# Last query chunk's output product in seven half-size products, and the fourth tile's end moved by one query group

## Chip, cores and metric

The kernel runs on one core of a Trainium2 chip. The metric is device time in microseconds (us) of one execution; where several were timed, their median. The profiled execution is one of them: its span is what the profile shows, from first to last instruction, and a little more lies around it. TensorE (PE in the profile) multiplies matrices, VectorE (DVE) and ScalarE (ACT) work on elements, GpSimd (POOL) and SyncE (SP) issue the DMAs here.

## The reference, cut to what matters

Attention with 16 query heads on 8 key/value heads over the last 512 keys, with a gated feed-forward branch on the same normalised input. The output is `x + s * g`.

```python
# x (1, 2048, 448); Hq = 16, Dh = 256, Hkv = 8, W = 512
xn = layernorm(x)
q  = (xn @ wq).reshape(1, 2048, 16, 256).transpose(0, 2, 1, 3)
p  = softmax(einsum("bhqd,bhkd->bhqk", q, k[last 512]) * 256 ** -0.5)
o  = einsum("bhqk,bhkd->bhqd", p, v[last 512])
s  = o.transpose(0, 2, 1, 3).reshape(1, 2048, 4096) @ wo      # 4096 x 448
g  = silu((gelu(xn @ w_gate) * (xn @ w_up)) @ w_down)
out = x + s * g
```

The change is in the product with `wo`, 2048 x 4096 times 4096 x 448.

## The kernel before

**An order written out by hand.** `Plan` (lines 39 to 166) records every operation in program order. Each engine runs its own operations in that order, and semaphore waits follow from who wrote and who reads each buffer. `K.reuse` (line 61) makes a new buffer wait for all users of the bytes that it overlaps. A DMA is an operation of the engine whose queue issues it: one that has to wait holds back everything behind it on that engine. All matmuls are recorded in line 370, all ScalarE copies in line 361, two-operand VectorE operations in line 364, plain DMAs in line 355 and transposing DMAs in line 358; one goes by tile names.

**Stages.** First comes the normalisation and the feed-forward branch, whose gate `g` goes to DRAM (`g2_all`, in the profile `g_all`) tile by tile, 16 tiles of 128 tokens. Then attention runs over `m` from 0 to 63 (line 906): four chunks of 512 tokens, 16 heads in each. `groups` (line 347) says at which `m` query projections are computed for the next 6 or 8 heads, two heads at a time (`q_group`, line 695). In each chunk after the first they stand at `m % 16 == 2` and `m % 16 == 10`. `s_mm(m)` (line 713) makes the scores of one head in the four banks `AB`, ScalarE takes the exponentials into `p32`, VectorE normalises them into `pn` (three buffers), and SP transposes `pn` into `pT` by DMA, two transposes for a head. `pv(m)` (line 734) multiplies by the values two heads later (`LAG = 2`), in two of the four banks `BB`. Its result goes to `oTh` in half precision, scaled by 64, for chunks 0 to 2, and to `oT` (the same bytes, bfloat16) for chunk 3. In a steady step TensorE does `s_mm(m)` and `pv(m - 2)`.

**The output product of chunks 0 to 2** is `burst(c)` (line 799), called at `m % 16 == 1` of the next chunk. It splits the chunk's tokens, the head dimension and 384 of the 448 output columns in two and needs seven half-size products in place of eight (`product`, line 786, in half precision, with weights `wt` prepared earlier). Four of the seven have sums of `oTh` as their operand; `sums(n)` (line 812) makes them on VectorE for four heads at a time into three buffers `sr`, which lie over `qT`, `pn` and `p32`. The other 64 columns are plain products with `w3` (line 846), in bank `BN`. Results come out transposed. `plus`, `part` and `fold` (lines 823 to 839) put them together in `xs` (the first chunk's columns of `xnT`), SP transposes `xs` by DMA into `sT` and `sN`, and `burst_end(c, t4)` (line 879) finishes a tile of tokens. It is called for tiles 0 to 2 within the query projections at `m % 16 == 2` and for tile 3 at `m % 16 == 3` (line 930).

**The output product of chunk 3** is plain: `wo_mm` (line 750), 32 pieces of the contraction for each of four tiles, the last tile split into 320 and 128 columns (lines 938 to 954). The first two tiles' pieces of heads 0 to 12 stand before or between the last two `pv`. Its weights `wo` (3.5 MB) go over the bytes of `wt` in four loads of 896 KB by POOL's queue (`load_wo`, line 895): two within the burst of chunk 2 (lines 853 and 861), one in the second projection step at m = 50 and one in the first step at m = 58 (line 913).

**The end of a tile** is `wo_end` (line 757), with `wo_fin` (line 772) for chunk 3:

```python
mult(g2[:, g, :], b_g2[g])                       # DVE: product with the gate
if t + NG2 < NT and c1 == D: load_g2(t + NG2)    # POOL queue; NG2 = 2
add("dve", xr[:, x, c0:c1], ...)                 # DVE: plus x
dma("sp" if t >= NT - 4 else "pool", out_view[:, t, c0:c1], xr[:, x, c0:c1], bx, ())
if t + NXR < NT and c1 == D:                     # NXR = 3, POOL queue
    dma("pool", xr[:, x, :], x_view[:, t + NXR, :], (), b_xr[x])
```

There are two buffers for the gate (`g2`) and three for `x` (`xr`, overwritten by the output). Tile 12 ends first in chunk 3, tile 15 last.

Of the kernel before, what the change touches and what calls it, by code (L numbers as in the profile page):

```python
# [168 lines left out]
def bass_recurrent_scan__sliding_block_cached__geglu_ffn__prompt_kernel(  # L169
# [41 lines left out]
    with es:  # L211
# [14 lines left out]
        def sbuf_bufs(at, size, n):  # L226
            return [K.buf(at + i * size, size) for i in range(n)]
# [53 lines left out]
        w3, _, rw_end = place("w3", [P, NCO, R], F16)  # L281
        w3b, _, _ = place("w3b", [P, NCO, R], BF16, at=a_w3)
        b_w3 = [K.buf(a_w3 + i * NCO // NB * R * 2, NCO // NB * R * 2) for i in range(NB)]
        wo, a, a2 = place("wo", [P, NCO, D], BF16, at=rw + 3 * Hq * N2 * 2)
        assert a2 <= rw_end
        b_wo = sbuf_bufs(a, 8 * D * 2, NCO // 8)
        x4, a, a2 = place("x4", [P, NT, D], BF16, at=rw)
        b_x4 = sbuf_bufs(a, D * 2, NT)
        NXN = 14
# [67 lines left out]
        def dma_t(o, i, reads=(), writes=()):  # L357
            K.op("sp", lambda e, o=o, i=i: e.dma_start_transpose(o, i), reads, writes, dma=True)
# [350 lines left out]
                     (b_ps[b + 1],), (b_qT[s][1],))  # L709

        AB, BB = [], []

        def s_mm(m):
            s, g = qs(m), m % Hq // 2
# [19 lines left out]
        def pv(m):  # L734
            h = m % Hq
            g, x = h // 2, m % NPT
            for e in range(2):
                b = BB[m % 2 * 2 + e]
                mms([(bank[b].rearrange("p (t q) -> p t q", q=P), va[:, g, j, e * P:(e + 1) * P],
                      pT[:, x, :, :, j, :].rearrange("p a t q -> p (a t) q"), j == 0, j == NJ - 1)  # L740
                     for j in range(NJ)], [b_va[g]] + b_pT[x], (b_ps[b],))
                i = 2 * h + e
                o, f = (oTh, WS) if m < NS - Hq else (oT, 1.0)
                if e == 0:
                    act(o[:, i, :], bank[b], ACT.Copy, (b_ps[b],), (b_oT[i],), scale=f)
                else:
                    K.op("dve", lambda v, i=i, b=b, o=o, f=f: v.tensor_scalar(  # L747
                        o[:, i, :], bank[b], f, None, op0=ALU.mult), (b_ps[b],), (b_oT[i],))

        def wo_mm(t4, b, lo, hi, c0=0, c1=D):  # L750
            ch = list(range(lo, hi))
            mms([(bank[b][:, c0:c1], oT[:, i, t4 * P:(t4 + 1) * P], wo[:, i, c0:c1], i == 0, i == NCO - 1)
                 for i in ch],
                [b_oT[i] for i in ch] + [b_wo[p] for p in sorted({i // 8 for i in ch})],
                (b_ps[b],))

        def wo_end(t, c0, c1, mult, bt, y):

# [23 lines left out]

        o_view = oTh.rearrange("p (h e) (r q) -> p e r h q", e=2, r=2)
        HALF = (slice(0, R), slice(R, P))

        def product(j, b, rhs, hs, first, reads):

# [11 lines left out]
        def burst(c):  # L799


            allh = list(range(Hq))
            A = lambda e, r: (lambda h: o_view[:, e, r, h, :])
            bA = lambda e, hs: [b_oT[2 * h + e] for h in hs]
            B1, B5, B3, B7 = BB
            B6, BN = AB[0], AB[1]
            F = 0.5 / (WS * WS)
            xs = [xnT[:, k, 0:QC] for k in range(4)]
            U2, U3 = tmp[:, 0, :], tmp[:, 1, :]
            K.reuse([b for x in b_sr for b in x] + [b for x in b_cc[2:] for b in x])  # L810

            def sums(n):
                hs = range(n * HB, (n + 1) * HB)
                t, bt = sr[n % 3], b_sr[n % 3]
                o = lambda e, r: o_view[:, e, r, hs.start:hs.stop, :]
                S = lambda i: t[:, i, :, :]
                for i, x, y, r, op in ((3, o(0, 0), o(0, 1), bA(0, hs), ALU.subtract),
                                       (2, o(1, 1), S(3), bA(1, hs) + [bt[3]], ALU.subtract),
                                       (0, S(2), o(0, 0), bA(0, hs) + [bt[2]], ALU.add),
                                       (1, o(1, 0), S(2), bA(1, hs) + [bt[2]], ALU.subtract)):  # L820
                    add("dve", S(i), x, y, r, (bt[i],), op)
# [18 lines left out]

            for n in range(3):
                sums(n)
            for hs in (allh[:Hq - 2], allh[Hq - 2:]):
                product(0, B1, A(0, 0), hs, hs[0] == 0, bA(0, hs))
            act(U2, bank[B1], ACT.Copy, (b_ps[B1],), b_tmp[0], scale=F)
            for lo, hi in ((0, NCO - 4), (NCO - 4, NCO)):
                mms([(bank[BN][HALF[u], 0:HC], w3[:, i, :], oTh[:, i, u * HC:u * HC + HC], i == 0, i == NCO - 1)
                     for i in range(lo, hi) for u in range(2)],
                    b_oT[lo:hi] + [b_w3[i] for i in sorted({i * NB // NCO for i in range(lo, hi)})], (b_ps[BN],))
            act(xs[3][:, 0:HC], bank[BN][:, 0:HC], ACT.Copy, (b_ps[BN],), b_xs[3:], scale=F)  # L850
            dma_t(sN[:, :, :], xs[3][:, 0:HC], b_xs[3:], (b_sN,))
            if c == NQC - 2:
                load_wo(3)
            for n in range(Hq // HB):
                for j, i, b in ((6, 3, B7), (5, 2, B6), (4, 0, B5), (2, 1, B3)):
                    product(j, b, lambda h, n=n, i=i: sr[n % 3][:, i, h % HB, :], allh[n * HB:(n + 1) * HB], n == 0, [b_sr[n % 3][i]])
                if n == 0:
                    sums(3)
            K.reuse([b for x in b_cc[:2] for b in x])
            if c == NQC - 2:  # L860
                load_wo(0)
            product(1, B1, A(1, 0), allh, False, bA(1, allh))
            part(B1, None, [], 0, 0, 2)
            plus(U2, B6, U2, b_tmp[0], b_tmp[0])
            plus(U3, B7, U2, b_tmp[0], b_tmp[1])
            product(3, B7, A(1, 1), allh, True, bA(1, allh))
            part(B5, U3, b_tmp[1], 1, 1, 3)
            plus(U2, B5, U2, b_tmp[0], b_tmp[0])
            part(B3, U2, b_tmp[0], 0, 1, 0)
            dma_t(sT[:, :, 1, :], xs[1], b_xs[1:2], (b_sT[1],))  # L870
            for r, n, slot in ((0, 0, 2), (1, 1, 3), (0, 1, 0)):
                fold(r, n, slot)
            part(B7, U3, b_tmp[1], 1, 0, 1)
            dma_t(sT[:, :, 0, :], xs[0], b_xs[0:1], (b_sT[0],))
            fold(1, 0, 1)
            dma_t(sT[:, :, 2, :], xs[2], b_xs[2:3], (b_sT[2],))
            K.reuse([b for y in b_qT for b in y])

        def burst_end(c, t4):
# [9 lines left out]
                    add("dve", at(y), i, at(g), reads + [bg], b_tmp[s], ALU.mult)  # L889
            wo_end(t, 0, D, mult, b_tmp[s], y)  # L890

        LAG = 2
        late = []

        def load_wo(i):
            K.reuse(b_wo[i:i + 1])
            dma("pool", wo[:, i * 8:(i + 1) * 8, :],
                A_wo.rearrange("(c p) d -> p c d", p=P)[:, i * 8:(i + 1) * 8, :], (), (b_wo[i],))

        NS = NQC * Hq  # L900
# [4 lines left out]
        BB.extend(bk(nxt, j) for j in range(4))  # L905
        for m in range(NS):
            if m in groups:
                for i in range(m, groups[groups.index(m) + 1], 2):
                    end = m > Hq and m % Hq == LAG
                    q_group(i, (cur, nxt)[((i - m) // 2 + (m == Q0 + QS)) % 2], end)  # L910
                    if end and i > m:
                        burst_end(m // Hq - 1, (i - m) // 2 - 1)
                    if m >= NS - Hq + LAG and i - m == (2 if end else 0):
                        load_wo(1 if end else 2)
                if m == 0:
                    K.reuse([b for x in b_pT for b in x] + b_pn + b_p32)
            if m > Hq and m % Hq == LAG:
                K.reuse(b_pn + b_p32)
            s_mm(m)
            if m < LAG:  # L920
                down(NQC - LAG + m, nxt)
                if m == LAG - 1:
                    K.reuse(b_oT + [b for y in b_qT[:QS - Q0] for b in y])
                    assert not CASTS and not SUMS
                    K.reuse(b_sT + [b_sN])
                    for t in range(NG2):
                        load_g2(t)
            if len(late) == LAG:
                pv(late.pop(0))
            if m > Hq and m % Hq == LAG + 1:  # L930
                burst_end(m // Hq - 1, 3)
            if m > Hq and m % Hq == LAG - 1:
                if m // Hq == 1:
                    for b in b_xs:
                        b.old.extend(y for t in range(4) for z in b_xnT[t] for y in z.readers + [z.writer])
                burst(m // Hq - 1)
            late.append(m)
        c = NQC - 1
        LATE = NCO - 2 * (LAG + 1)
        wo_mm(0, AB[0], 0, LATE)  # L940
        pv(late.pop(0))
        pv(late.pop(0))
        wo_mm(1, AB[1], 0, LATE)
        wo_mm(0, AB[0], LATE, NCO)
        wo_fin(c, 0, AB[0])
        wo_mm(1, AB[1], LATE, NCO)
        wo_fin(c, 1, AB[1])
        wo_mm(2, AB[2], 0, NCO)
        wo_fin(c, 2, AB[2])
        for i in range(2):  # L950
            b = (AB[3], BB[0])[i]
            lo, hi = ((0, CUT), (CUT, D))[i]
            wo_mm(3, b, 0, NCO, lo, hi)
            wo_fin(c, 3, b, lo, hi)

        K.schedule()

# [52 lines left out]
```

## Time and profile before

| what | value |
|---|---|
| median of 5 runs | 560.87 us (560.24 to 562.68) |
| the profiled execution's own time | 560.24 us |
| its span | 558.4 us |
| TensorE busy (matmuls) | 546.6 us, 98% of the span |
| VectorE, ScalarE, GpSimd busy | 346.5, 309.8, 44.6 us |
| mean granted TensorE clock | 0.997 |
| chain that ended last | PE 92%, DMA 4%, DVE 2%, ACT 1%, issue 1% |

The span is divided in 40 slices of 14 us in the page's second part; each digit is the busy share in tenths. The chain that ended last is followed back from the last instruction to what released it at each step. A row of the timeline gives start, length, engine, line, operation and tiles, and in brackets the idle time before it and what ended it. Matmul ends are modelled, so starts are the better measure. A few matmul records are missing. Times below without another word are us from the start of the span.

### The profile page before, as it was taken

How to read it: one execution, taken by the hardware profiler on the slowest of the kernel's cores; microseconds unless marked ns; L12 is line 12 of the kernel's file. 1: busy time of each engine (PE TensorE's matmuls, PEld its weight loads, DVE VectorE, ACT ScalarE, POOL GpSimd, SP SyncE). 2: the span in 40 equal slices, each digit the busy share in tenths (PEclk: the TensorE clock that was granted, in tenths of full speed). 3: DMA queues.
4: the chain of work that ended last, by engine and by line, in shares of the span. 5: the costliest groups of instructions: out<-in, count | busy, mean ns of one | idle time of the engine just before them, and what ended most of it. 6: DMA issues, size and time to landing. Idle time of an engine off the chain costs nothing.

```text
span 558.4 us, 11469 instructions
## 1 busy us (share of the span) xinstructions
PE 546.6 (98%) x4444; PEld 288.5 (52%) x4444; DVE 346.5 (62%) x804; ACT 309.8 (55%) x783; POOL 44.6 (8%) x83
## 2 busy tenths in 40 slices
PE   9999999999999999999999999999999999599997
PEld 5554444445444444974444489444446954244455
DVE  6664635763547758756766795487578747456722
ACT  5434536753558668037857831687586058557700
POOL 1141500000000000003100000310000113100000
PEclk9999999999999999999999999999999999999999
DMA  9666399903307726325943830397076348952702
GB/s 292 121 185 142 87 273 272 162 20 93 87 20 151 151 39 158 37 31 130 166 106 67 161 83 17 79 185 151 14 153 138 97 87 221 183 114 65 144 19 59
DMA packets 177766, 66.46 MB, mean 119 GB/s; under 512 B 159856, under 2 KB 173680, under 8 KB 177712
## 3 DMA queue, kind: packets, MB, share of 16 engines
q1 hardware_dynamic: 172960, 52.76, 45.5%
q0 software_dynamic: 3984, 12.39, 8.2%
q8 instruction: 35, 0.57, 0.5%
q10 hardware_dynamic: 768, 0.57, 0.3%
q14 instruction: 19, 0.16, 0.1%
HBM read 23.43 MB, written 3.67 MB: 49 GB/s over the span
## 4 chain that ended last, share of the span: by engine, by line
PE 92%; DMA 4%; DVE 2%; ACT 1%; issue 1%; ACTq 0%; DVEq 0%
PE bank L370 91%; DMA pT<-pn 4%; ACT p L721 1%; DVE pn L728 1%; PE bank L487 1%; ACT qT L361 0%; DVE oTh L747 0%; DVE rden L725 0%; PE bank L468 0%; DVE tmp L778 0%; DVE xr L364 0%; DVE gl L400 0%; DVE epst L401 0%; ACTq L155 0%; DVE oT L747 0%
## 5 line engine op out<-in xcount | busy, mean ns | idle before, releaser
L721 ACT ACTIVATE p<-bank 128x512 f32<-128x512 f32 x256 | 150.7, 596 | 33.6 <-DVE pn L728 25.8
L370 PE MATMUL bank<-pT,va 128*128 128x512 bf16 x512 | 122.0, 382 | 7.2 <-DMA pT<-pn 7.2
L370 PE MATMUL bank<-kT,qT 128*128 128x512 bf16 x512 | 121.7, 381 | 0.0
L728 DVE TENSOR_SCALAR pn<-p,rden 128x512 bf16<-128x512 f32 x256 | 113.1, 484 | 13.1 <-DMA pT<-pn 8.9
L370 PE MATMUL bank<-xnT,wq 64*128 64x512 bf16 x768 | 94.9, 376 | 0.5 <-DVE oTh L747 0.5
L370 PEld LDWEIGHTS bank<-pT,va 128*128 128x128 bf16 x512 | 49.6, 98 | 69.7 <-DMA pT<-pn 11.1
L370 PE MATMUL bank<-xnT,wgu 64*128 64x512 bf16 (+2 forms) x768 | 83.9, 350 | 0.1
L370 PEld LDWEIGHTS bank<-kT,qT 128*128 128x128 bf16 x512 | 49.6, 98 | 62.9 <-issue 4.8
L361 ACT ACTIVATE qT<-bank 128x512 bf16<-128x512 f32 x76 | 44.1, 596 | 54.1 <-PE bank L370 52.5
L708 DVE CAST qT<-bank 128x512 bf16<-128x512 f32 x52 | 35.1, 692 | 47.5 <-PE bank L370 47.4
L370 PEld LDWEIGHTS bank<-xnT,wq 64*128 64x128 bf16 x768 | 36.7, 94 | 47.1 <-ACT p L721 1.7
L370 PEld LDWEIGHTS bank<-xnT,wgu 64*128 64x128 bf16 x768 | 37.2, 94 | 36.9 <-issue 0.7
L536 DVE TENSOR_TENSOR actT<-bank,gl 128x512 bf16<-128x512 f32 x56 | 37.8, 690 | 26.5 <-PE bank L370 19.9
L361 ACT ACTIVATE gl<-bank 128x512 bf16<-128x512 f32 x56 | 33.2, 597 | 37.0 <-PE bank L370 34.9
L725 DVE RECIPROCAL rden<-rsum 128x2 f32<-128x2 f32 x128 | 21.2, 165 | 50.2 <-ACT p L721 50.0
L721 ACT ACTIVATION_READ_ACCUMULATOR p<-bank 128x1 f32 x256 | 51.4, 201 | 0.0
L370 PE MATMUL bank<-wd,actT 128*128 128x448 bf16 x224 | 43.0, 353 | 0.0
L355 POOL DMA_DIRECT2D g<-g_all x16 | 8.7, 542 | 348.9 <-DVE tmpb L364 285.7
L747 DVE TENSOR_SCALAR oTh<-bank 128x512 f16<-128x512 f32 x48 | 32.8, 683 | 0.0
L370 PEld LDWEIGHTS bank<-wd,actT 128*128 128x128 bf16 x224 | 21.8, 98 | 21.1 <-issue 0.4
L370 PE MATMUL bank<-sr,wt 128*64 128x256 f16 x576 | 31.9, 273 | 0.0
L370 PEld LDWEIGHTS bank<-sr,wt 128*64 128x64 f16 x576 | 31.5, 110 | 0.0
(63 smaller groups left out, 415.9 us busy)
## 6 DMA issues: line engine op xcount, KB each, us to landing
wo<-in_A_wo_dram POOLq DMA_DIRECT2D x4, 896.0 KB, 5.9
wtb<-in_A_wo_dram POOLq DMA_DIRECT2D x4, 768.0 KB, 7.4
wq<-in_A_wq_dram SPq DMA_DIRECT2D x2, 1536.0 KB, 11.3
va<-in_A_v_cache_dram SPq DMA_DIRECT2D x8, 256.0 KB, 5.3
pT<-pn SPq DMA_TRANSPOSE x128, 2.8
g_all<-g2w SPq DMA_DIRECT2D x16, 112.0 KB, 2.1
xr<-in_A_x_dram POOLq DMA_DIRECT2D x16, 112.0 KB, 2.6
g<-g_all POOLq DMA_DIRECT2D x16, 112.0 KB, 2.6
```

The source lines that it names most:

```text
L355: K.op(q, lambda e, o=o, i=i: e.dma_start(o, i), reads, writes, dma=True)
L361: K.op("act", lambda e, o=o, i=i: e.activation(o, i, func, scale=scale), reads, writes)
L370: ins = e.matmul(o, lhsT=l, rhs=r, start=st, stop=sp, skip_group_check=True)
L487: ins = e.matmul(bank[b][:, 0:w], lhsT=gl[:, 0, 0:P], rhs=gl[:, 0, 0:w], start=True, stop=True)
L536: K.op("dve", lambda e: e.tensor_tensor(actT[:, c % 2, f, :], bank[b + 1], gl[:, s, :], ALU.mult), (b_ps[b + 1], b_gl[s]), (b_actT[c % 2][ ...
L708: K.op("dve", lambda v, s=s, b=b: v.tensor_copy(qT[:, s, 1, :], bank[b + 1]), (b_ps[b + 1],), (b_qT[s][1],))
L721: K.op("act", lambda e, b=b, r=r, z=z: e.activation(p32[:, z, :], bank[b], ACT.Exp, scale=att_scale, accum_out=rsum[:, r:r + 1]), (b_ps[b] ...
L725: K.op("dve", lambda e, r=r: e.reciprocal(rden[:, r - 1:r + 1], rsum[:, r - 1:r + 1]), b_rsum[r - 1:r + 1], b_rden[r - 1:r + 1])
L728: K.op("dve", lambda e, r=r - 1 + t, z=(n - 1 + t) % NP32, y=y, t=t: e.tensor_scalar(pn[:, y, t, :], p32[:, z, :], rden[:, r:r + 1], None, ...
L747: K.op("dve", lambda v, i=i, b=b, o=o, f=f: v.tensor_scalar(o[:, i, :], bank[b], f, None, op0=ALU.mult), (b_ps[b],), (b_oT[i],))
```

## The change

The burst is now used for chunk 3 too, for heads 0 to 13. It stands after the loop, ahead of the last two `pv`; there the `w3` product is issued later, behind the seventh product, and the results are not transposed by DMA: `turn` transposes them with small matmuls against `ident` straight into PSUM, and `wo_mm` adds the last two heads' four pieces (`NL = 4`) on top. `wo` is 448 KB and loaded once, by POOL's queue, over the weights of product 0, as soon as that product of the last burst is done. The four `load_wo` are gone. For heads 0 to 13 of chunk 3 `pv` writes scaled half precision. The last burst's factor is 1.0 in place of 0.5, since `wo_fin` multiplies by 0.5. `burst_end(c, 3)` of chunks 0 to 2 goes from m % 16 == 3 to the second projection step at m % 16 == 10. In query groups of six heads (m = 12 and m = 58) the three steps use other PSUM banks.

```diff
@@ placement
-        wo, a, a2 = place("wo", [P, NCO, D], BF16, at=rw + 3 * Hq * N2 * 2)
-        b_wo = sbuf_bufs(a, 8 * D * 2, NCO // 8)
+        NL = 4
+        wo, a, a2 = place("wo", [P, NL, D], BF16, at=rw + WAT[0] * Hq * N2 * 2)
+        b_wo = K.buf(a, NL * D * 2)
@@ pv
-                o, f = (oTh, WS) if m < NS - Hq else (oT, 1.0)
+                o, f = (oTh, WS) if m < NS - LAG else (oT, 1.0)
@@ wo_mm, turn
+        def wo_mm(t4, b, c0=0, c1=D):
+            mms([(bank[b][:, c0:c1], oT[:, i, t4 * P:(t4 + 1) * P], wo[:, i - NCO + NL, c0:c1], False, i == NCO - 1)
+                 for i in range(NCO - NL, NCO)], b_oT[NCO - NL:] + [b_wo], (b_ps[b],))
+
+        def turn(t4, b, c0=0, c1=D):
+            tok = slice(t4 * P, (t4 + 1) * P)
+            lst = [(0, 0, tok, slice(0, P)), (P, 2, tok, HALF[0]), (N2, 1, tok, slice(0, P)), (N2 + P, 2, tok, HALF[1]),
+                   (2 * N2, 3, slice(t4 % 2 * P, t4 % 2 * P + P), HALF[t4 // 2])]
+            lst = [x for x in lst if c0 <= x[0] < c1]
+            mms([(bank[b][:, lo:lo + k.stop - k.start], xs[j][:, q], ident[:, k], i == 0, False)
+                 for i, (lo, j, q, k) in enumerate(lst)], b_xs + [b_ident], (b_ps[b],))
@@ burst
-            allh = list(range(Hq))
+            last = c == NQC - 1
+            NH = Hq - (LAG if last else 0)
+            NCH = 2 * NH
+            allh = list(range(NH))
-            F = 0.5 / (WS * WS)
+            F = (1.0 if last else 0.5) / (WS * WS)
...
-                hs = range(n * HB, (n + 1) * HB)
+                hs = range(n * HB, min((n + 1) * HB, NH))
...
             act(U2, bank[B1], ACT.Copy, (b_ps[B1],), b_tmp[0], scale=F)
-            if c == NQC - 2:
-                load_wo(3)
+            if last:
+                K.reuse([b_wo])
+                dma("pool", wo[:, :, :], A_wo.rearrange("(c p) d -> p c d", p=P)[:, NCO - NL:NCO, :], (), (b_wo,))
+            def plain():
+                for lo, hi in ((0, NCH - 4), (NCH - 4, NCH)):
+                    mms([(bank[BN][HALF[u], 0:HC], w3[:, i, :], oTh[:, i, u * HC:u * HC + HC], i == 0, i == NCH - 1)
+                         for i in range(lo, hi) for u in range(2)],
...
+                act(xs[3][:, 0:HC], bank[BN][:, 0:HC], ACT.Copy, (b_ps[BN],), b_xs[3:], scale=F)
+            def turned(k):
+                if not last:
+                    if k == 3:
+                        dma_t(sN[:, :, :], xs[3][:, 0:HC], b_xs[3:], (b_sN,))
+                    else:
+                        dma_t(sT[:, :, k, :], xs[k], b_xs[k:k + 1], (b_sT[k],))
+            if not last:
+                plain()
+                turned(3)
             for n in range(Hq // HB):
...
-            if c == NQC - 2:
-                load_wo(0)
             product(1, B1, A(1, 0), allh, False, bA(1, allh))
...
             product(3, B7, A(1, 1), allh, True, bA(1, allh))
+            if last:
+                plain()
@@ main loop
-                    q_group(i, (cur, nxt)[((i - m) // 2 + (m == Q0 + QS)) % 2], end)
-                    if m >= NS - Hq + LAG and i - m == (2 if end else 0):
-                        load_wo(1 if end else 2)
+                    p = (i - m) // 2
+                    q_group(i, ((cur, nxt[::-1], (cur[1], nxt[1])) if three else (cur, nxt) * 2)[p], end)
+                    if m > Hq and m % Hq == LAG + QS and p == 1:
+                        burst_end(m // Hq - 1, 3)
-            if m > Hq and m % Hq == LAG + 1:
-                burst_end(m // Hq - 1, 3)
@@ after the loop
+        burst(c)
         pv(late.pop(0))
         pv(late.pop(0))
...
+        ends = [(0, AB[2], 0, D), (1, AB[3], 0, D), (2, AB[0], 0, D), (3, AB[1], 0, CUT), (3, BB[0], CUT, D)]
+        for t4, b, c0, c1 in ends[:3]:
+            turn(t4, b, c0, c1)
+        for i, (t4, b, c0, c1) in enumerate(ends):
+            if i >= 3:
+                turn(t4, b, c0, c1)
+            wo_mm(t4, b, c0, c1)
+            wo_fin(c, t4, b, c0, c1)
```

More of the change, by code (lines that the diff above doesn't have):

```diff
@@ L283, in bass_recurrent_scan__sliding_block_cached__geglu_ffn__prompt_kernel @@
         b_w3 = [K.buf(a_w3 + i * NCO // NB * R * 2, NCO // NB * R * 2) for i in range(NB)]
-        wo, a, a2 = place("wo", [P, NCO, D], BF16, at=rw + 3 * Hq * N2 * 2)
-        assert a2 <= rw_end
-        b_wo = sbuf_bufs(a, 8 * D * 2, NCO // 8)
+        NL = 4
+        wo, a, a2 = place("wo", [P, NL, D], BF16, at=rw + WAT[0] * Hq * N2 * 2)
+        assert NL * D <= Hq * N2
+        b_wo = K.buf(a, NL * D * 2)
         x4, a, a2 = place("x4", [P, NT, D], BF16, at=rw)
@@ L711, in bass_recurrent_scan__sliding_block_cached__geglu_ffn__prompt_kernel @@
         AB, BB = [], []
+        LAG = 2
+        NS = NQC * Hq
         def s_mm(m):
@@ L748, in pv @@
                         o[:, i, :], bank[b], f, None, op0=ALU.mult), (b_ps[b],), (b_oT[i],))
[L750 to L755, printed above, removed]
+        def wo_mm(t4, b, c0=0, c1=D):
[8 more added lines that the diff above has]
+                 for i, (lo, j, q, k) in enumerate(lst)], b_xs + [b_ident], (b_ps[b],))
         def wo_end(t, c0, c1, mult, bt, y):
@@ L784, in bass_recurrent_scan__sliding_block_cached__geglu_ffn__prompt_kernel @@
         HALF = (slice(0, R), slice(R, P))
+        xs = [xnT[:, k, 0:QC] for k in range(4)]
         def product(j, b, rhs, hs, first, reads):
@@ L806, in burst @@
             B6, BN = AB[0], AB[1]
-            F = 0.5 / (WS * WS)
-            xs = [xnT[:, k, 0:QC] for k in range(4)]
+            F = (1.0 if last else 0.5) / (WS * WS)
             U2, U3 = tmp[:, 0, :], tmp[:, 1, :]
@@ L812, in sums @@
             def sums(n):
-                hs = range(n * HB, (n + 1) * HB)
+                hs = range(n * HB, min((n + 1) * HB, NH))
                 t, bt = sr[n % 3], b_sr[n % 3]
                 o = lambda e, r: o_view[:, e, r, hs.start:hs.stop, :]
-                S = lambda i: t[:, i, :, :]
+                S = lambda i: t[:, i, 0:len(hs), :]
                 for i, x, y, r, op in ((3, o(0, 0), o(0, 1), bA(0, hs), ALU.subtract),
@@ L842, in burst @@
                 sums(n)
-            for hs in (allh[:Hq - 2], allh[Hq - 2:]):
+            for hs in (allh[:NH - 2], allh[NH - 2:]):
                 product(0, B1, A(0, 0), hs, hs[0] == 0, bA(0, hs))
             act(U2, bank[B1], ACT.Copy, (b_ps[B1],), b_tmp[0], scale=F)
[L846 to L851, printed above, removed]
-            if c == NQC - 2:
-                load_wo(3)
+            if last:
[5 more added lines that the diff above has]
+                         for i in range(lo, hi) for u in range(2)],
+                        b_oT[lo:hi] + [b_w3[i] for i in sorted({i * NB // NCO for i in range(lo, hi)})], (b_ps[BN],))
+                act(xs[3][:, 0:HC], bank[BN][:, 0:HC], ACT.Copy, (b_ps[BN],), b_xs[3:], scale=F)
[8 more added lines that the diff above has]
+                turned(3)
             for n in range(Hq // HB):
+                hs = allh[n * HB:(n + 1) * HB]
                 for j, i, b in ((6, 3, B7), (5, 2, B6), (4, 0, B5), (2, 1, B3)):
-                    product(j, b, lambda h, n=n, i=i: sr[n % 3][:, i, h % HB, :], allh[n * HB:(n + 1) * HB], n == 0, [b_sr[n % 3][i]])
+                    product(j, b, lambda h, n=n, i=i: sr[n % 3][:, i, h % HB, :], hs, n == 0, [b_sr[n % 3][i]])
                 if n == 0:
@@ L869, in burst @@
             part(B3, U2, b_tmp[0], 0, 1, 0)
-            dma_t(sT[:, :, 1, :], xs[1], b_xs[1:2], (b_sT[1],))
+            turned(1)
             for r, n, slot in ((0, 0, 2), (1, 1, 3), (0, 1, 0)):
@@ L873, in burst @@
             part(B7, U3, b_tmp[1], 1, 0, 1)
-            dma_t(sT[:, :, 0, :], xs[0], b_xs[0:1], (b_sT[0],))
+            turned(0)
             fold(1, 0, 1)
-            dma_t(sT[:, :, 2, :], xs[2], b_xs[2:3], (b_sT[2],))
+            turned(2)
             K.reuse([b for y in b_qT for b in y])
@@ L890, in burst_end @@
             wo_end(t, 0, D, mult, b_tmp[s], y)
-        LAG = 2
         late = []
[L895 to L900, printed above, removed]
         act(tmp[:, 1, 0:1], nhalf[:, :], ACT.Exp, (b_nhalf,), (b_tmp[1][0],))
@@ L907, in bass_recurrent_scan__sliding_block_cached__geglu_ffn__prompt_kernel @@
             if m in groups:
-                for i in range(m, groups[groups.index(m) + 1], 2):
+                hi = groups[groups.index(m) + 1]
+                three = hi - m == 6
+                for i in range(m, hi, 2):
                     end = m > Hq and m % Hq == LAG
-                    q_group(i, (cur, nxt)[((i - m) // 2 + (m == Q0 + QS)) % 2], end)
-                    if end and i > m:
-                        burst_end(m // Hq - 1, (i - m) // 2 - 1)
-                    if m >= NS - Hq + LAG and i - m == (2 if end else 0):
-                        load_wo(1 if end else 2)
+                    p = (i - m) // 2
+                    q_group(i, ((cur, nxt[::-1], (cur[1], nxt[1])) if three else (cur, nxt) * 2)[p], end)
+                    if end and p:
+                        burst_end(m // Hq - 1, p - 1)
+                    if m > Hq and m % Hq == LAG + QS and p == 1:
+                        burst_end(m // Hq - 1, 3)
                 if m == 0:
@@ L938, in bass_recurrent_scan__sliding_block_cached__geglu_ffn__prompt_kernel @@
         c = NQC - 1
-        LATE = NCO - 2 * (LAG + 1)
-        wo_mm(0, AB[0], 0, LATE)
+        burst(c)
         pv(late.pop(0))
         pv(late.pop(0))
[L943 to L954, printed above, removed]
+        ends = [(0, AB[2], 0, D), (1, AB[3], 0, D), (2, AB[0], 0, D), (3, AB[1], 0, CUT), (3, BB[0], CUT, D)]
[6 more added lines that the diff above has]
+            wo_fin(c, t4, b, c0, c1)
         K.schedule()
```

## The prediction

> **What bounds the kernel now.** I read the slices first, then the waits, then the timeline around each gap of TensorE.
>
> ```profile
> PE   9999999999999999999999999999999999599997
> ...
> DMA  9666399903307726325943830397076348952702
> ```
>
> TensorE is full except in slice 35 (474.6 to 488.6) and at the end. So only three things can count: TensorE work, that gap, and what lies behind the last matmul. The list of waits names the gap's releaser (total, times, longest):
>
> ```profile
> PE bank L370 <- DMA pT<-pn: 7.2, 5, 4.3
> ```
>
> TensorE waits for the transposes of `pn`. I took the eight heads from the first `s_mm` after the burst to the next projections in each of the three chunk transitions (columns: start:end, length, busy time of PE, PEld, DVE, ACT, POOL, granted clock, DMA share, GB/s); the fourth row is 16 matmuls behind the longest gap:
>
> ```profile
> 256.43:284.95 28.52, 27.95 (x130) 12.29 (x128) 21.66 (x62) 24.87 (x75) 3.96 (x7) 1.00 0.78 161
> 359.04:387.76 28.72, 27.99 (x130) 12.26 (x130) 21.77 (x62) 24.87 (x75) 3.80 (x7) 1.00 0.79 162
> 461.83:497.65 35.82, 29.94 (x130) 12.64 (x129) 21.65 (x61) 25.01 (x75) 5.14 (x9) 0.95 0.90 182
> 487.23:492.38 5.15, 5.15 (x17) 2.01 (x18) 2.62 (x6) 2.48 (x8) 0.00 (x0) 0.67 0.73 163
> ```
>
> The same work takes 7.2 us longer in the third transition than in the mean of the others (28.62). A steady head takes 3.45 us (494.10 to 497.55), eight 27.6, so all three lose something: 0.9, 1.1 and 8.2. In the third the timeline has
>
> ```profile
> 479.08 0.90 POOL L355 DMA_DIRECT2D wo<-in_A_wo_dram  x1
> ...
> 487.23 3.00 PE L370 MATMUL bank<-pT,va 128*128 128x512 bf16 x8 [4.32 <-DMA pT<-pn]
> ```
>
> The transpose issued at 479.40 landed after 7.8 us, while steady ones take 2.7. The gap then costs clock (0.67 in the fourth row): 5.15 us in place of 3.45. An earlier wait of 1.33 us (479.28) belongs to a transpose of 472.4 that took 6.0 us; its neighbours are the gate load (472.12) and the output (472.65, 5.5 us to landing) of the fourth tile's end. In the other transitions, too, the one stall (0.57, 0.73) belongs to a transpose of 4.6 to 4.8 us next to that tile's end.
>
> **The product itself.** The third burst, by starts on TensorE:
>
> ```profile
> 427.68 2.81 PE L370 MATMUL bank<-oTh,wt 128*64 128x256 f16 x48
> 430.33 3.66 PE L370 MATMUL bank<-oTh,w 128*64 128x256 f16 x64
> 433.82 10.65 PE L370 MATMUL bank<-sr,wt 128*64 128x256 f16 x192
> 444.30 5.41 PE L370 MATMUL bank<-oTh,wt 128*64 128x256 f16 x96
> 449.64 0.82 PE L370 MATMUL bank<-xnT,wq 64*128 64x512 bf16 x6
> ```
>
> 16 heads take 2.65 + 3.49 + 10.48 + 5.34 = 21.96 us; 14 heads, 7/8 of each: 2.32 + 3.05 + 9.17 + 4.67 = 19.2. The plain product has 96 matmuls of 448 columns at 187 ns (549.48 less 543.4 is about 6.0 for 32), 32 of 320 at 136 (549.48 to 553.83) and 32 of 128 at 55 (553.83 to 555.62): 24 us.
>
> **The tail's end, before:**
>
> ```profile
> 542.29 0.62 DVE L778 SCALAR_TENSOR_TENSOR tmp<-bank,g 128x448 f32<-128x448 f32 x1 [5.36 <-PE bank L370]
> ...
> 543.22 0.55 POOL L355 DMA_DIRECT2D g<-g_all  x1 [63.23 <-DVE tmp L778]
> ...
> 546.62 0.54 POOL L355 DMA_DIRECT2D xr<-in_A_x_dram  x1 [2.85 <-DMA out_dram<-xr]
> 547.15 0.54 POOL L355 DMA_DIRECT2D g<-g_all  x1
> ...
> 553.83 0.49 DVE L778 SCALAR_TENSOR_TENSOR tmp<-bank,g 128x320 f32<-128x320 f32 x1 [3.06 <-PE bank L370]
> ```
>
> This is a chain of transfers hidden under TensorE. Tile 12's multiplication starts at M = 542.29. Its output, issued by SP at 543.61, must land before POOL may load `x` for tile 15 into the same buffer (M + 4.33), and tile 15's gate stands behind that load in POOL's queue (M + 4.86). It lands 3.2 us after its issue, at M + 8.06. Tile 15 needs it at 553.83, M + 11.5: 3.5 us of slack, because two tiles of plain product lie between.
>
> **The change, part by part.**
>
> 1. *Four `wo` loads go.* The excess of the third transition, 7.2 us with the clock loss, goes with them (bounds: 4, if the 1.33 us wait and its late `pn` stay; 8.2, if nothing is left). The loads within the burst of chunk 2 had no gap beside them: 0.
>
> 2. *The fourth tile's end moves.* Its four VectorE operations (1.4 us) and its gate load, output and `x` load (POOL, 0.55 us each) leave the place where transposes are short of time. At the new place VectorE has two casts of 1.34 us in steps of 3.03 (503.26, 506.29), so 1.4 us fits, and POOL is empty. Nothing waits behind them: tiles 13's and 14's loads are needed 40 us later. Gain from 0 (tile 2's transfers are still near, and the burst of transposes itself is dense) to 2.7 (the losses of 0.9, 1.1 and the third's last 1.0 all gone less the usual 0.1 each). The nearest rows are the two idle times, 0.57 and 0.73; I take half of each and as much in the third: **1.0**. If VectorE did not fit, each of three steps would lose at most 1.4.
>
> 3. *The last burst starts at 527.67, where the plain product started.* Without `w3` in front, the summed products follow product 0 at once, so VectorE's sums lose a cover of 3.49 us. In the third burst the first sum starts 1.49 us after the burst's first matmul (429.17) and a set of four takes 2.66; TensorE needs 10.48 / 4 = 2.62 for a set's products. First sum ready at +2.17, product 0 ends at +2.32; from there each product is at or up to 0.1 behind its sum. I add 0.1. The lower bound is 0; the upper, if each of 15 sums is awaited with a semaphore delay of 0.1, is 1.5. The third set lies over `pn` and waits for the last transpose; the like one in the third burst, issued about +1.0 and landing about +4, is in time for a sum that starts at +6.8.
>
> 4. *`wo`, 448 KB,* is issued after product 0 (about +2.7) and lands within 5.9 us (what 896 KB took). It is needed at +24: 15 us of slack. On POOL only the tail's loads stand behind it. Cost 0; were it to hold the last transpose by as much as 896 KB did (5 us), the third set would be 2 to 3 us late.
>
> 5. *Putting together.* VectorE's and ScalarE's last pieces follow product 3 by 1.5 to 2 us (449.75 to 451.48 for product 3's end at 449.6). The `w3` product behind it takes 3.05, so `xs` and the four `BB` banks are free when `pv` comes: cost 0; without that cover 2.
>
> 6. *Two `pv`* take 3.45 (532.59 to 536.04), the last evacuation starts 0.2 later and takes 0.69. Before, they stood within the product, so they are no new work; the wait for their `pT` was covered by 26 plain matmuls and is now by the burst.
>
> 7. *`turn`:* 15 matmuls of 128 or 64 columns before the first `wo_mm`, 5 later. The nearest row is the 55 ns of a 128-column matmul with its weights: 0.83 us, beside the evacuation of 0.9. The Trainium skill (TensorE: Matmul & The Clock Gate, Part 4: PE-mode transpose) speaks against this: it gives about 275 ns for a transpose of 128 x 128 in a kernel, so 15 would take 4.1 and M be 3.2 later. I take the row: these are ordinary matmuls with the identity as moving operand, and eight such on 64 rows took 0.28 us (start of the trace).
>
> 8. *`wo_mm`:* four matmuls of 187 ns are 0.75, and VectorE starts 0.25 after (the same for M before: 536.04 + 32 x 0.187 = 542.0).
>
> The new M: 527.67 + 19.2 + 0.1 + 3.45 + 0.9 + 0.05 + 0.75 + 0.25 = **552.4**, 10.1 later than before. But tiles 13 to 15 follow on TensorE within 2.6 us, so now the transfer chain is late next. Tile 12 and 13 follow each other on VectorE as before (542.29, 543.50), so its lengths are taken as they are: gate of tile 15 at M + 8.1, four operations of 0.53 + 0.52 + 0.32 + 0.29 = 1.66, then 2.17 from the last VectorE operation (556.23) to the span's end. The end is M + 11.9 = **564.3**, 5.9 later than 558.4. The skill's page on DMA (DMA: Bandwidth & Descriptors, Anatomy of one DMA) puts a transfer at a fixed 2.0 us plus its bytes; three transfers of 112 KB by that estimate would be shorter than the 2.5 and 3.2 us here, and tile 15 would start about 1.3 us earlier, at M + 6.8. The trace has these very transfers, so it decides.
>
> 9. *Hidden edits.* Other banks for groups of six: before `s_mm(58)` TensorE has no gap above 0.05 us (506.89, 506.94), so 0, at most 0.1 either way. `pv`'s scaled write: 683 ns on VectorE both ways. The factor: 0.
>
> **Sum.** -7.2 - 1.0 + 5.9 = -2.3: span 556.1, own time 557.9 where the profiled run had 560.24. That run is the fastest of five; the median lies 0.63 above, so the forecast is **558.6**.
>
> **Rivals.**
> - *All stalls go* (gains of 8.2, 0.9 and 1.1, less the 0.1 that remains at each projection): -9.9 + 5.9 = -4.0, time 556.9. For it: each stall in the trace has a transfer of the changed parts beside it. Against: a head's first transposes come closer together than in the steady state, whatever else moves.
> - *Slower: the late transposes of the third transition are not the loads' doing.* DMA share is 0.78 there without any load of `wo`. If the transpose of 472.4 is late again and `pn` with it, and the next takes 5 us, only about 3 of the 8.2 are gained and the tail's 5.9 decide: +2.9, time 563.8. It turns slower by over 0.3% when the gain is under 4.2. Against: 7.8 us to landing fits the 7.3 us of the load issued 0.3 us before.
> - *No change:* the turns at the skill's price. Only the first 15 count, the others lie beside the chain: +3.2 on M, time 561.8.
>
> **From these to the numbers.** 0.3% of 560.87 is 1.7 us, about what a measurement of this kernel tells from none. Forecast 0.52, with its own range of 557.0 to 560.6 from the bounds of 1, 2 and 3, of which 0.34 is faster and 0.17 the same, 0.01 slower; all stalls go 0.22, faster; slower 0.20; turns or late sums 0.06, half the same and half slower. Together: faster 0.56, same 0.20, slower 0.24. The range must reach into both sides: 555.6 to 562.8.
>
> **What would show it.** Third transition near 28.6 us or below, at clock 1.00. No idle TensorE from 427 on until the last burst is over, `pv` about 19.3 us after its first matmul. At the end, TensorE done some 9 us before the span ends, and VectorE idle for about 4 us before tile 15, with the gate or `x` load as what ended it. I would be wrong if transposes stay above 5 us in the third transition, if TensorE waits for `sr`, or if tile 15 doesn't wait.

## The result and the profile after

| | before | changed |
|---|---|---|
| median | 561.05 us (47 runs) | 557.37 us (26 runs) |
| ratio | 1 | 0.9943 (95% interval 0.9932 to 0.9953) |
| profiled execution, own time | 560.24 us | 557.42 us |
| its span | 558.4 us | 555.6 us |

The kernel is 0.57% faster by the ratio. The forecast was 558.6 us; the measured 557.37 us is 1.2 us lower and inside the forecast's range.

The page's first rows and slices, changed kernel:

```profile
PE 543.8 (98%) x4674; PEld 294.6 (53%) x4674; DVE 361.3 (65%) x833; ACT 313.1 (56%) x791; POOL 41.3 (7%) x80
...
PE   9999999999999999999999999999999999999992
```

Slice 35 is full now, and the idle time has gone to the last slice. The same stretches as before: the three transitions, then from the burst's start to M, the first multiplication of tile 12 on VectorE, then from M to the end (start:end, length, busy PE, PEld, DVE, ACT, POOL, clock, DMA share, GB/s):

```profile
255.73:283.70 27.97, 27.91 (x131) 12.29 (x130) 20.88 (x58) 24.98 (x75) 2.19 (x4) 1.00 0.76 152
358.03:385.76 27.73, 27.73 (x130) 12.37 (x129) 20.97 (x58) 24.98 (x75) 2.15 (x4) 1.00 0.75 155
459.89:488.23 28.34, 27.91 (x131) 12.30 (x130) 20.77 (x57) 24.91 (x75) 2.15 (x4) 1.00 0.78 146
518.22:543.64 25.42, 24.92 (x388) 21.06 (x388) 17.89 (x35) 4.49 (x11) 0.76 (x1) 1.00 0.19 46
543.64:555.60 11.96, 2.44 (x21) 1.48 (x19) 5.13 (x10) 0.00 (x0) 1.61 (x3) 0.72 0.25 68
```

In the kernel before, the product took this up to M, and this up to the end:

```profile
527.67:542.29 14.62, 14.62 (x77) 7.33 (x76) 3.01 (x6) 1.63 (x3) 0.00 (x0) 1.00 0.28 38
527.67:558.40 30.73, 27.91 (x177) 15.85 (x175) 8.24 (x16) 1.63 (x3) 1.62 (x3) 1.00 0.23 45
```

In the changed kernel the stretch behind M is the new bound: TensorE works for 2.44 of 11.96 us, VectorE for 5.13. The timeline of this stretch says what VectorE waits for:

```profile
543.64 0.62 DVE L788 SCALAR_TENSOR_TENSOR tmp<-bank,g 128x448 f32<-128x448 f32 x1 [1.03 <-PE bank L371]
...
547.21 0.62 DVE L788 SCALAR_TENSOR_TENSOR tmp<-bank,g 128x448 f32<-128x448 f32 x1 [1.09 <-DMA g<-g_all]
...
548.00 0.54 POOL L356 DMA_DIRECT2D xr<-in_A_x_dram  x1 [2.89 <-DVE tmp L788]
548.52 0.54 POOL L356 DMA_DIRECT2D g<-g_all  x1
551.91 0.49 DVE L788 SCALAR_TENSOR_TENSOR tmp<-bank,g 128x320 f32<-128x320 f32 x1 [3.41 <-DMA g<-g_all]
```

Tile 14 waits 1.09 us for its gate, and tile 15 waits 3.41 us for its own, the last link of the chain that TensorE used to hide. (The wait of POOL at 548.00 is named after VectorE. In the same row of the profile before, the output of tile 12 is named; I take it that it came last here too.)

Where the time went, by starts on TensorE in the two profiled executions:

| stretch | before | changed | difference |
|---|---|---|---|
| up to the first transition | 256.43 | 255.73 | -0.70 |
| three transitions | 28.52, 28.72, 35.82 | 27.97, 27.73, 28.34 | -0.55, -0.99, -7.48 |
| the stretches between them, up to the last product | | | +0.27 |
| last product's start to tile 12's first multiplication (M) | 14.62 | 25.42 | +10.80 |
| M to the span's end | 16.11 | 11.96 | -4.15 |
| sum | 558.4 | 555.6 | -2.8 |

So 9.45 us were gained ahead of the last product, and 6.65 given back from its start to the end. These are single executions; by the medians the gain is 3.7 us.

### The profile page after: what moved, and what is told of

It is laid out like the page before. It is cut to its first block, busy times and chain, and to the rows that moved or that the text cites. A ratio compares the mean times of both kernels' runs of the same rounds, so it can differ in the third digit from the quotient of the medians.

```text
span 555.6 us, 11965 instructions
## 1 busy us (share of the span) xinstructions
PE 543.8 (98%) x4674; PEld 294.6 (53%) x4674; DVE 361.3 (65%) x833; ACT 313.1 (56%) x791; POOL 41.3 (7%) x80
## 4 chain that ended last, share of the span: by engine, by line
PE 89%; DMA 4%; DVE 3%; ACT 2%; issue 1%; POOL 0%; DVEq 0%; ACTq 0%; POOLq 0%
PE bank L371 88%; DMA pT<-pn 3%; ACT p L724 2%; DVE pn L731 1%; DMA g<-g_all 1%; PE bank L488 1%; DVE rden L728 0%; DVE tmp L788 0%; DVE xnT L365 0%; DVE oT L750 0%; ACT cc L362 0%; DVE xr L365 0%; PE bank L469 0%; DVE sr L365 0%; DVE oTh L750 0%
## 5 line engine op out<-in xcount | busy, mean ns | idle before, releaser
L750 DVE TENSOR_SCALAR oTh<-bank 128x512 f16<-128x512 f32 x62 | 42.4, 683 | 0.0
L371 PE MATMUL bank<-sr,wt 128*64 128x256 f16 x744 | 41.5, 273 | 0.1
L371 PEld LDWEIGHTS bank<-sr,wt 128*64 128x64 f16 x744 | 40.1, 110 | 1.0 <-DVE sr L365 0.3
L362 ACT ACTIVATE xnT<-bank 128x256 bf16<-128x256 f32 (+2 forms) x12 | 4.9, 417 | 63.2 <-PE bank L371 62.4
```

The lines of the kernel that those rows point to most:

```text
L362: K.op("act", lambda e, o=o, i=i: e.activation(o, i, func, scale=scale), reads, writes)
L371: ins = e.matmul(o, lhsT=l, rhs=r, start=st, stop=sp, skip_group_check=True)
L750: K.op("dve", lambda v, i=i, b=b, o=o, f=f: v.tensor_scalar(o[:, i, :], bank[b], f, None, op0=ALU.mult), (b_ps[b],), (b_oT[i],))
```

## The experiments

Each ratio is taken against runs of the kernel before on the same chip. The kernel before had medians from 560.49 to 561.24 us there, so a difference of under 1 us between two medians says little where the intervals of the ratios overlap. "Own" numbers come from the one profiled execution.

**The load of `wo`.** First alone, in the kernel before, by holding it back:

```diff
 def load_wo(i):
-    dma("pool", wo[:, i * 8:(i + 1) * 8, :], ...)
+    held = [o for o in K.ops if o.eng == "pe"][-1:] if i == 2 else []
+    K.op("pool", ..., dma=True, after=held)
```

> The kernel before, but the third load of wo (896 KB, issued at 479 us) waits for the first query projections of m = 58 (about 500 us), when no transposes of the loop are due. Theory (this load makes the transposes late and costs the gap of 4.3 us and the slow clock behind it): the third transition takes 29 to 31 us in place of 35.8, time 5 to 6.5 us below 561. Rival (transposes are late there by themselves or by the fourth tile's transfers): the transition stays above 34 us, time within 1.5 us of 561.

Measured: 554.89 us, ratio 0.9900 (0.9883 to 0.9917), the third transition:

```profile
462.32:492.88 30.56, 28.08 (x131) 12.28 (x130) 21.48 (x61) 24.82 (x75) 4.21 (x8) 1.00 0.90 184
```

The granted clock is 1.00 where it was 0.95, and the length 30.56 where it was 35.82. POOL's row shows that the load was in fact held (496.38, behind the transition's end at 492.88):

```profile
480.69 1.90 PE L370 MATMUL bank<-pT,va 128*128 128x512 bf16 x8 [1.39 <-DMA pT<-pn]
496.38 0.90 POOL L898 DMA_DIRECT2D wo<-in_A_wo_dram  x1 [15.64 <-PE bank L370]
```

The gap of 4.32 is gone; two waits of 1.09 and 1.39 us are left, at the place where the fourth tile's end still stood. Holding back one transfer gives about 1.0%, more than the whole change.

Then the reverse, a load put into the changed kernel:

```diff
+if m == NS - Hq + 6:
+    held = [o for o in K.ops if o.eng == "pe"][-3:-2]
+    K.op("pool", lambda e: e.dma_start(wod[:, :, :], A_wo.rearrange("(c p) d -> c p d", p=P)[0:8, :, :]), ..., dma=True, after=held)
```

> The changed kernel with one transfer added: 896 KB of wo copied to a DRAM buffer that nobody reads, on the same queue, issued behind s_mm(54) where the third load of wo fell before. Theory (such a transfer beside the transposes costs the gap): the third transition grows from 28.3 us by 4 to 7 us, time 561 to 564. Rival: it stays within 1 us of 28.3.

Measured: 562.21 us, ratio 1.0030 (1.0016 to 1.0043), 4.8 above the changed kernel. Its profiled execution was the fastest of twelve (559.85), and there the transition took 31.21 us, 2.9 more than in the changed kernel:

```profile
475.76 0.54 POOL L956 DMA_DIRECT2D wo_copy<-in_A_wo_dram  x1 [10.79 <-PE bank L371]
...
482.22 1.90 PE L371 MATMUL bank<-pT,va 128*128 128x512 bf16 x8 [2.91 <-DMA pT<-pn]
```

The gap comes right behind the transfer, with the transposes as releaser. Both directions agree: the transfer beside the transposes is the cause. The copy goes to DRAM and not to the core's own memory, so it is not exactly the old load; the transition of the profiled run fell short of the 4 us expected, the median did not.

**The fourth tile's end,** put back in the changed kernel:

```diff
-                    if m > Hq and m % Hq == LAG + QS and p == 1:
-                        burst_end(m // Hq - 1, 3)
+            if m > Hq and m % Hq == LAG + 1:
+                burst_end(m // Hq - 1, 3)
```

> The changed kernel, but the fourth tile's end of chunks 0 to 2 is back at m % 16 == 3. Theory (its transfers and VectorE work make the transposes of the first heads late): the transitions take 28.5, 28.7 and some 29 us again in place of 28.0, 27.7 and 28.3, time 1.5 to 2.5 us above 557.4. Rival (the shorter transitions come from elsewhere or are chance): within 0.5 us of 557.4.

Measured: 560.04 us (557.94 to 565.52 in 12 runs), ratio 0.9993 (0.9969 to 1.0018). That is 2.7 us above the changed kernel, slightly more than expected, and the scatter is twice as wide. Own transitions: 28.13, 28.61, 31.82, in an execution (561.66) that is slower than the median. The third:

```profile
470.66 0.74 POOL L356 DMA_DIRECT2D out_dram<-xr  x1
...
478.64 2.71 PE L371 MATMUL bank<-pT,va 128*128 128x512 bf16 x8 [2.24 <-DMA pT<-pn]
```

No `wo` load is near, and TensorE still waits 2.24 us and then runs 16 matmuls in 5.15 us (478.64 to 483.79) in place of 3.45. So the tile's end costs time without the load beside it. What the runs don't separate is its three transfers from its four VectorE operations, which moved together. And in the last 2 us before the wait ends the trace has another neighbour, the fetch of 16 KB of the program's own instructions (queue q8):

```profile
q1 hardware_dynamic: 161, 0.04, 133.7%
q8 instruction: 1, 0.02, 3.4%
```

The section at the end comes back to it.

**The banks of the groups of six,** old ones in the changed kernel:

```diff
-q_group(i, ((cur, nxt[::-1], (cur[1], nxt[1])) if three else (cur, nxt) * 2)[p], end)
+q_group(i, (cur, nxt)[(p + (m == Q0 + QS)) % 2], end)
```

> The changed kernel with the old PSUM banks for the query groups of six heads. Theory (at m = 12 the second pair of heads had to wait for an evacuation of pv in the bank that it used, 0.69 us): the stretch up to the first burst is 0.7 us longer, time 0.7 us above 557.4. Rival (chance of one execution): no difference.

Measured: 558.16 us, ratio 0.9960 (0.9945 to 0.9976), 0.8 above the changed kernel. The intervals overlap, so the profile says more than the median: the first transition starts at 256.39 and not 255.73, so the stretch is 0.66 longer. The rows at m = 12, first of the kernel before, then of this run:

```profile
193.15 0.82 PE L370 MATMUL bank<-xnT,wq 64*128 64x512 bf16 x6 [0.53 <-DVE oTh L747]
193.11 0.82 PE L371 MATMUL bank<-xnT,wq 64*128 64x512 bf16 x6 [0.53 <-DVE oTh L750]
```

The first projections used the banks of `pv`, whose evacuation was still to come. With the new banks that matmul starts at 192.46, 0.69 earlier than before.

**The tail's transfers.** The gates of tiles 14 and 15 and `x` of tile 15 go early into the bytes of `sT`, which are free from m = 58 on:

```diff
+gx, _, _ = place("gx", [P, 3, D], BF16, at=a_s)
...
+if m // Hq == NQC - 1:
+    K.reuse(b_gx + b_x15)
+    for t in (NT - 2, NT - 1):
+        dma("pool", gx[:, t - NT + 2, :], g2d[t], (b_g2d[t],), (b_gx[t - NT + 2],))
+    dma("pool", gx[:, 2, :], x_view[:, NT - 1, :], (), b_x15)
```

> The changed kernel, but the gate of tiles 14 and 15 and x of tile 15 are loaded into the bytes of sT, once tile 11 is done with them (m = 58), so that nothing at the end waits for a transfer. Theory (the chain output 12, x 15, gate 15 sets the end): from the first multiplication of tile 12 to the span's end about 7.4 us in place of 12.0, time about 4.6 us below the changed kernel's 557.4, so 552.8. Rival (the end is set by VectorE or TensorE, the chain lies beside it): at most 1 us below.

Measured: 552.81 us, ratio 0.9866 (0.9839 to 0.9894), 4.6 below the changed kernel, as expected. M to the end, in its profiled execution:

```profile
546.70:554.00 7.30, 2.44 (x21) 1.47 (x19) 4.95 (x10) 0.00 (x0) 0.00 (x0) 1.00 0.20 64
```

7.30 us where the changed kernel needs 11.96. VectorE is the bound: its ten operations follow without a gap from 546.70 to 551.82. The start is late in this execution (its own time, 555.79, is the slowest of five), since the first transition took 29.8: it had one wait of 1.93 us for a transpose. Such waits still come in some executions (one of 2.15 in the profile of the `w3` run below).

**ScalarE's order in the last burst:**

```diff
-                act(xs[3][:, 0:HC], bank[BN][:, 0:HC], ACT.Copy, ...)      (in plain)
...
             part(B7, U3, b_tmp[1], 1, 0, 1)
+            if last:
+                plain_out()
```

> The changed kernel, but ScalarE's copy of the w3 result in the last burst stands behind its other pieces of that burst, not ahead of three of them. Theory (ScalarE holds back VectorE's pieces by 4.6 us until the w3 product is done, and the last evacuation for heads 14 and 15 is late by that): the second evacuation ends 0.3 to 0.5 us sooner after the burst's start, time 0.3 to 0.5 us below 557.4. Rival (the evacuation is bound by the pv matmuls): no difference.

Measured: 557.27 us, ratio 0.9945 (0.9925 to 0.9964), against 557.37 for the changed kernel: no difference that counts. In the profile the order does what it should. Changed kernel, ScalarE:

```profile
533.38 0.41 ACT L362 ACTIVATE cc<-cc 64x256 f32<-64x256 f32 x1
538.04 0.38 ACT L362 ACTIVATE xnT<-bank 128x256 bf16<-128x256 f32 x1 [4.24 <-PE bank L371]
538.43 0.72 ACT L362 ACTIVATE cc<-cc 64x256 f32<-64x256 f32 x2
```

and with the other order:

```profile
533.63 1.16 ACT L362 ACTIVATE cc<-cc 64x256 f32<-64x256 f32 x3
```

Two copies no longer stand behind the one that waits for the `w3` product, and from the last set of sums to M it takes 15.30 us in place of 15.63. But in this execution the sums began 0.5 later (a transpose ahead of them on VectorE, 0.87 us), so M itself came 25.59 after the burst's start, not sooner than 25.42. With the early transfers in place the same edit was tried once more:

> The changed kernel with the early loads for tiles 14 and 15 and with ScalarE's copy of the w3 result behind its other pieces. If both are on the path one after the other, the gains add: 4.6 + 0.4, time about 552.4. If the order of copies no longer counts once VectorE sets the end, it is as without it, about 552.8.

Measured: 552.60 us, ratio 0.9862 (0.9844 to 0.9880); e1's is 0.9866 (0.9839 to 0.9894). Whether the 0.3 us add can't be told from these runs.

**`w3` ahead of the sums' products again:**

```diff
-            if not last:
-                plain()
-                turned(3)
+            plain()
+            turned(3)
...
-            if last:
-                plain()
```

> The changed kernel, but in the last burst the w3 product stands where it stands in the other bursts, ahead of the products of sums. Theory of the prediction (VectorE's last pieces need its cover behind product 3): up to 2 us are added between the burst's end and the last wo products, less the 0.2 us that TensorE waits for sums now. Rival (pv of head 14 covers them, since its banks come free first): no loss, and with ScalarE not held back 0.3 to 0.6 us below 557.4.

Measured: 556.68 us, ratio 0.9926 (0.9905 to 0.9948), 0.7 below the changed kernel, with intervals that overlap. In the profile M comes 24.61 after the burst's start, 0.8 sooner. In the changed kernel the sums start 1.82 after the burst (a transpose holds VectorE for 0.37) and product 0's successor has to wait for them:

```profile
520.78 9.31 PEld L371 LDWEIGHTS bank<-sr,wt 128*64 128x64 f16 x168 [0.34 <-DVE sr L365]
```

With `w3` in between it doesn't. Behind product 3 nothing is lost: there `pv` follows at once, while VectorE reads the last pieces.

**Both tail edits together:**

> The changed kernel with the early loads for tiles 14 and 15 and the w3 product ahead of the products of sums. If e3's gain of 0.7 us adds to e1's of 4.6: about 552.1 us, with 24.6 us from the burst's start to the first multiplication of tile 12 and 7.3 from there to the end. It should still lie 1 to 2 us above the plain product with the same rest, since 24.6 + 7.3 is more than 30.7.

Measured: 552.02 us, ratio 0.9840 (0.9826 to 0.9854). From the burst's start to M, and from M to the end:

```profile
518.42:543.03 24.61, 24.42 (x388) 21.76 (x388) 18.08 (x36) 4.62 (x11) 0.76 (x1) 1.00 0.22 51
543.03:550.30 7.27, 2.44 (x21) 1.47 (x19) 4.95 (x10) 0.00 (x0) 0.00 (x0) 0.88 0.20 64
```

**The plain product with all the rest of the change.** The held load, the moved tile's end and the new banks in the kernel before:

```diff
+held = [o for o in K.ops if o.eng == "pe"][-1:] if i == 2 else []
...
-q_group(i, (cur, nxt)[((i - m) // 2 + (m == Q0 + QS)) % 2], end)
+q_group(i, ((cur, nxt[::-1], (cur[1], nxt[1])) if three else (cur, nxt) * 2)[p], end)
...
+if m > Hq and m % Hq == LAG + QS and p == 1:
+    burst_end(m // Hq - 1, 3)
...
-if m > Hq and m % Hq == LAG + 1:
-    burst_end(m // Hq - 1, 3)
```

> The kernel before with everything of the change but the new product: the plain output product of chunk 3 stays, its third load of wo waits for the first projections of m = 58, the fourth tile's end is one query group later, and the groups of six use the new banks. Theory (the change gained only beside the product, and the new product with its end costs 6.7 us more than the plain one): from the loop's last pv to the span's end 30.7 us as before, transitions of 28 us each, time 550 to 551. Rival (the seven products save TensorE time that counts): not below the changed kernel's 557.4.

Measured: 551.15 us, ratio 0.9817 (0.9804 to 0.9831), the lowest median of all. Its transitions were about 27.8, 28.0 and 29.3 us, where 28 each had been expected. Its last stretch, from the product's start to the end:

```profile
519.24:550.00 30.76, 27.91 (x177) 15.85 (x175) 8.24 (x16) 1.63 (x3) 1.61 (x3) 0.99 0.19 44
```

30.76 us, as in the kernel before (30.73), against 37.38 in the changed kernel and 31.88 in the best version of the new product. So the new product of the change costs 6 to 7 us (6.2 by the medians, 7.1 by the ratios). Mended at both ends it still loses about 1 us: 0.9 by the medians on one chip, at the edge of the noise, and 1.1 in the profiles. It keeps TensorE busy for 26.9 us in the mended version (24.42 + 2.44), in place of 27.9, which is little saved. Against that stands its end, 7.27 us behind M with 2.44 us of TensorE in them, for VectorE must finish four tiles there. The plain product finishes tile after tile and hides three of the four ends.

## Why the prediction held, point by point

- **The four loads (step 1), -7.2.** The mechanism is shown, by taking one load away and by adding one; the size is too large. The third transition became 7.48 shorter by this and step 2 together, and e5 gives 5.3 of it to the third load alone. The wait of 1.33 us, counted here, is one of those that stayed in e5 (1.39). It was also misread in part: the transpose issued at 472.4 held VectorE (478.49), while TensorE's wait ended with the next one, issued at 474.0 and landed after 5.2 us.
- **The fourth tile's end (step 2), -1.0.** That it costs time at its old place is right, the term too small: e4 puts 2.7 us on it in the median, at the upper bound given (2.7). I had taken half of TensorE's idle time in two transitions. The profile before could not show what this place costs in the third, where the loads' waits lay on top of it, and one execution doesn't show how often its waits are longer. The instruction fetch that falls in each of the three transitions was not looked at.
- **Hidden edits (step 9), 0.** Wrong for the banks: 0.69 us in the profile, and e7's median fits (0.8). I looked at m = 58 only. The wait stood in the profile, as an idle time of 0.5 us behind `DVE oTh` in the costly groups, and the other group of six at m = 12 was not looked up.
- **The sums' cover (step 3), 0.1.** The products of sums started 2.56 after the burst's start, not 2.32, and took 9.41 in place of 9.17: 0.5 us. VectorE stood behind a transpose before the first sum, which the burst taken as the model didn't show. So one of the signs of being wrong, TensorE waiting for `sr`, did come, but only for 0.34 us.
- **Putting together (step 5), 0.** The copies on ScalarE run in order, and the `w3` copy was issued ahead of two of them; this held VectorE's pieces until 538.9 and the last evacuation with them (0.3 us by e2's profile). "Without that cover 2" is refuted by e3: without it M came 0.8 us sooner.
- **The turns (step 7).** 15 took 0.77 us (0.83 from the 55 ns row), 51 ns each. The about 275 ns of the Trainium skill (TensorE: Matmul & The Clock Gate, Part 4: PE-mode transpose) are given for TensorE's transpose mode; these ordinary matmuls against an identity don't cost that, so the row was the right one to take. No run here uses the transpose mode for them.
- **The chain at the end (step 8).** M to the end: 11.9 forecast, 11.96 measured, with tile 15 at M + 8.3 (8.1 forecast), and e1 took the transfers away and got the 4.6 us, close to the waits of 1.09 and 3.41. The step from the product's start to M was 25.42 where 24.73 had been worked out; the 0.7 are for the most part the two steps above.

In sum -2.3 was forecast for the profiled execution and -2.8 measured: 1.25 more gained ahead of the product (transitions 0.8, banks 0.7, other stretches -0.27), 0.75 more lost from there on. Of the 1.2 us between the forecast median and the measured one, these 0.5 are one part. The other 0.7 is the 0.63 that was added because the run profiled before lay below its median; the changed kernel's profiled run lies at its median (557.42 and 557.37). The number came close partly by luck: the loads' term was too large and the tile end's too small, and what the transitions and banks gained beyond the forecast was more than half used up from the last product on.

The rival of a slower kernel fell with e5 and e6; that of the turns with the 0.77 us. The rival "all stalls go" (9.9 us off the transitions) can't be told from the forecast (8.2) by this execution: the transitions, now 27.7 to 28.3, gave 9.0, midway.

## What to carry to other kernels

Work that is taken off the busiest engine may have hidden a chain of transfers: before shortening a last stage, list the buffers that its ends reuse and the loads that wait behind each other on one queue. A change of several parts can be faster although its main part is a loss; time the parts alone, here a single wait put on one load gave more than the whole. And a large load wants a wait of its own where an in-order queue would let it out among transfers that are due soon: the third load went out at 479.08, though its place in the program is the projection step that TensorE began at 497.65.

## What the runs showed of the hardware

After a gap of 2.24 us in e4 TensorE's next 16 matmuls ran slow, with a granted clock of 0.62 from 480 to 484; after a longer one of 2.91 in e6 it stayed at 1.00 from 478 to 486. So the length of one gap alone did not decide here.

A transpose can also land late with no plain transfer beside it. In e1's first transition, which took 29.8 us where the changed kernel's took 28.0, the only neighbour between 264 and 266.5 is an instruction fetch:

```profile
266.46 1.90 PE L374 MATMUL bank<-pT,va 128*128 128x512 bf16 x8 [1.93 <-DMA pT<-pn]
...
GB/s 258 221 537 229 172 254 266 279 209 106 94 45 4 0 0 0 0 0 0 0 0 0 0 0 0 0 8 8 8 8 8 12 8 8 12 8 8 12 111 270
...
q8 instruction: 1, 0.02, 3.7%
```

The slices are 0.06 us each: the transpose's last packets trickle at 8 to 12 GB/s, and the wait ends when they are through. The same trickle stands behind a fetch in e4 ahead of its wait of 2.24, and in the kernel before ahead of the 0.73 and the 1.33. The changed kernel's profile has the fetch at 264 too, and there only VectorE waits (0.91 us). So the fetch is a likely part of these waits, beside the tile's end; no run took it away, and why it stops TensorE in one execution and not in another stays open. It is not part of the large gap: between 479 and 488 in the kernel before there is no fetch, and the load of `wo` is there.
